# Cosine attention and a GELU layer on one core: the order of the squares in the first batch, and row sums with one chunk halved by queries

## The chip, the core and the metric

The kernel runs on one core of one Trainium2 chip. The time is that of the device in microseconds, the median of several executions. A profile is one execution taken by the hardware profiler.

## What is computed

There are 8 batches of 12 heads, 448 positions and 64 numbers per head. The queries q and keys k are divided by their norms, scores are divided by tau = 0.1, a softmax is taken over the keys, and the values v are averaged with it. The heads side by side (768 numbers for each of 8 x 448 = 3584 tokens) then go through two matrix products with a GELU between them:

```python
q_n = q / (np.linalg.norm(q, axis=-1, keepdims=True) + 1e-06)
k_n = k / (np.linalg.norm(k, axis=-1, keepdims=True) + 1e-06)
attn = np.exp(np.matmul(q_n, k_n.transpose(0, 1, 3, 2)) / tau)   # the reference takes the row maximum off first
out = np.matmul(attn / np.sum(attn, axis=-1, keepdims=True), v)
x = out.transpose(0, 2, 1, 3).reshape(3584, 768)
h = x @ w_in                                  # 768 x 2048
result = (0.5 * h * (1 + erf(h / sqrt(2)))) @ w_out   # 2048 x 768
```

## The kernel before

**Tiles.** Four heads make a "quad" (`g`, three to a batch, 24 in all). A quad's q and k lie in one tile of 128 partitions: two heads (`h`) on the partition halves, two pairs of them (`s`) on the free axis, and the 448 positions as 7 chunks of 64 (`c`). A "unit" is what is normalised at once: units 0 and 1 are the two halves of quad 0, unit `u` from 2 on is quad `u - 1`.

**From q and k to scores.** For each unit: `square` (L147) squares q and k, `reduce` (L158, VectorE) adds the squares up, `logs` and `roots` (L169, L174, ScalarE) take the root as exp(0.5 ln x), `inverses` (L183) adds 1e-6 (on VectorE in the first batch, on GpSimd later) and takes the reciprocal on VectorE, `scale` (L200) multiplies q and k with it on GpSimd or VectorE into bf16, and the result is transposed, in the first batch by TensorE with a copy by VectorE (`transposes` L214, `copies` L227), later by a DMA that SyncE issues (L220). `scores` (L236) are 64x64 matmuls, four of which run side by side in the array; `exps` (L250, ScalarE) take the exponential of two banks at a time (128 x 896).

**From exponentials to x.** `sums` (L259) multiplies each chunk of exponentials with a matrix of ones. In later batches that matrix has 32 columns, so that four such matmuls stand side by side in the array, in column strips `r` = 0, 32, 64 and 96: for `s` = 0 and 1, even chunks go into one strip and odd chunks into the other, and the two are added afterwards (`inverted` L296). `turned` (L291) transposes the sums, `inverted` takes reciprocals, `spread` (L312) spreads them out again, and `normalise` (L317) multiplies them into the output of `values` (L274, 64x64 matmuls), all on VectorE. `both` (L321) issues the whole of this for one quad.

**Order.** Nothing is scheduled by a planner: each engine runs its instructions in the order in which the program issues them. `attention_first` (L401) is the first batch, written out by hand. `attention` (L581) is a later batch: its scores are cut into eight `group`s (L575) of two or three passes over three pairs of PSUM banks (`group_pairs`, L573), and between them `run` (L586) issues matmuls of the second layer of the batch before (`second_pieces`, L339; 16 of them make one half row block, which VectorE then copies out, L352). `plan` (L583) gives the numbers of these filling matmuls: six runs, 96 in all in batches 1, 3, 5 and 7, and 128 in batches 2, 4 and 6. In `attention`, `both` of the batch's first quad follows group 2, that of the second follows group 5, and that of the third follows the last run. Three pairs of banks serve scores and, in turn, the values: pair 0 for the first quad, pair 1 for the others. `first` (L621) is the first layer of a batch with its GELUs; it begins with `scale` and `transposes` for the next batch.

`upto(f, n)` (L390) calls `f` for all numbers below `n` that have not been done. In `attention`, `upto(root, 2 * b + 5)` (L617) computes the norms of the next batch's first two quads: logs, roots and inverses, ahead of the last run.

Of the kernel before, what the change touches and what calls it, by code (L numbers as in the profile page):

```python
# [16 lines left out]
def kernel(  # L17
# [17 lines left out]
    nc = tc.nc  # L35
    B, H, S, D = q.shape
    C = S // D
# [35 lines left out]
    ones = consts.tile([128, 32], BF16)  # L73
# [25 lines left out]
    def mm_tile(name, shape=(128, 512), dtype=F32, aside=None):  # L99
        t = ps_mm.tile(list(shape), dtype, tag=f"mm{turn[0] if aside is None else turn[0] ^ aside}", name=name)  # L100
        if aside is None:
            turn[0] ^= 1
        return t
# [10 lines left out]
    groups = [[n] for n in range(NQ + 2)] + [[NQ + 2, NQ + 3]]  # L114
# [4 lines left out]
    qk_t, v_t, sq_t, nq_t, rn_t, qkb_t, qkT_t, pt_t = {}, {}, {}, {}, {}, {}, {}, {}  # L119
# [27 lines left out]
    def square(u, parts=None):  # L147
        g, s0, s1 = units[u]
        if g not in sq_t:
            sq_t[g] = sqp.tile([128, 2, 2, C, D], F32, tag="sq", name=f"sq{g}")  # L150
        sq, t = sq_t[g][:, :, s0:s1], qk_t[g][:, :, s0:s1]
        for eng, part in parts or ((nc.gpsimd, slice(0, 2)),):
            if eng is nc.scalar:
                eng.activation(sq[:, part], t[:, part], AF.Square)
            else:
                eng.tensor_tensor(sq[:, part], t[:, part], t[:, part], ALU.mult)  # L156

    def reduce(u, part=slice(0, 2)):  # L158
        g, s0, s1 = units[u]
        sq = sq_t[g][:, :, s0:s1]  # L160
        n, j = place[u]
        if n not in nq_t:
            nq_t[n] = nrm.tile([128, len(groups[n]), 2, s1 - s0, C], F32, tag="nq", name=f"nq{n}")
        nq = nq_t[n][:, j]
        nc.vector.tensor_reduce(nq[:, part], sq[:, part], mybir.AxisListType.X, ALU.add)  # L165
# [3 lines left out]
    def logs(n):  # L169
        nq = nq_t.pop(n)  # L170
        ln_t[n] = nrm.tile(list(nq.shape), F32, tag="lq", name=f"lq{n}")
        nc.scalar.activation(ln_t[n], nq, AF.Ln, bias=tiny)

    def roots(n):  # L174
        ln = ln_t.pop(n)
        if n <= NQ:
            sr_t[n] = root2[n % len(root2)][:, :math.prod(shapes[n])]
            nc.scalar.activation(sr_t[n][:, :, 0], ln.rearrange("p j i s c -> p (j i s c)"), AF.Exp, scale=0.5)
        else:
            sr_t[n] = nrm.tile(list(ln.shape), F32, tag="sr", name=f"sr{n}")  # L180
            nc.scalar.activation(sr_t[n], ln, AF.Exp, scale=0.5)  # L181

    def inverses(n):  # L183
        sr = sr_t.pop(n)
        shape = [128] + shapes[n]
        se = nrm.tile(shape, F32, tag="se", name=f"se{n}")
        if n <= NQ:
            nc.vector.tensor_reduce(se.rearrange("p j i s c -> p (j i s c)"), sr, mybir.AxisListType.X, ALU.add)
        else:
            nc.gpsimd.tensor_scalar(se, sr, 1e-6, None, ALU.add)  # L190
        rn = nrm.tile(shape, F32, tag="rn", name=f"rn{n}")
        nc.vector.reciprocal(rn, se)  # L192
        rn_t[n] = rn
# [20 lines left out]
    def transposes(u, i=None):  # L214
        g, s0, s1 = units[u]
        qkb = qkb_t[g]
        if g not in qkT_t:
            qkT_t[g] = qkTp.tile([128, 2, C, 128], BF16, tag="qkT", name=f"qkT{g}")
        if i is None:
            nc.sync.dma_start_transpose(out=qkT_t[g].rearrange("p i c s -> p (i c) s"),  # L220
                                        in_=qkb.rearrange("p i c s d -> p (i c s d)"))
            return
        tp = tp_t[u, i] = mm_tile(f"tp{u}_{i}", (128, C, 128), BF16)
        for c in range(C):
            nc.tensor.transpose(tp[64 * s0:64 * s1, c, :], qkb[:, i, c, s0:s1].rearrange("p s d -> p (s d)"), ident)  # L225
# [31 lines left out]
    bank_t = {}  # L257

    def sums(g, chunks=range(C)):  # L259
        for c in chunks:  # L260
            if c == 0:
                bank_t[g, "sm"] = ps_acc.tile([128, 512], F32, tag="sm", name=f"sm{g}") if g < NQ else \
                    mm_tile(f"sm{g}", aside=0)
            for s in range(2):
                if g < NQ:
                    nc.tensor.matmul(bank_t[g, "sm"][64 * s:64 * (s + 1), :S],  # L266
                                     lhsT=ones2.rearrange("p a h r -> p (a h r)"), rhs=pt_t[g, s, c],
                                     start=(c == 0), stop=(c == C - 1), tile_position=(0, 64 * s))
                    continue
                r = 32 * (2 * s + c % 2)  # L270
                nc.tensor.matmul(bank_t[g, "sm"][r:r + 32, :S], lhsT=ones, rhs=pt_t[g, s, c],  # L271
                                 start=(c < 2), stop=(c >= C - 2), tile_position=(0, r))

    def values(g, chunks=range(C), p=None):  # L274
        for c in chunks:
# [15 lines left out]
    def turned(g):  # L291
        tr = rcp.tile([128, NB, 32], F32, tag="tr", name=f"tr{g}")
        nc.vector.transpose(tr.rearrange("p b r -> p (b r)"), bank_t.pop((g, "sm"))[:, :S])  # L293
        bank_t[g, "tr"] = tr.rearrange("p b (k r) -> p k b r", k=2)

    def inverted(g):  # L296
        tr = bank_t.pop((g, "tr"))
        if g < NQ:
            su = tr[:, :, :, 0]
        else:  # L300


            for j in range(4):
                o = j ^ 1
                nc.vector.tensor_reduce(tr[32 * j:32 * (j + 1), :, :, 1], tr[32 * o:32 * (o + 1), :, :, 0:1],  # L305
                                        mybir.AxisListType.X, ALU.add)
            su = rcp.tile([128, 2, NB], F32, tag="su", name=f"su{g}")
            nc.vector.tensor_reduce(su, tr[:, :, :, 0:2], mybir.AxisListType.X, ALU.add)
        rc = bank_t[g, "rc"] = rcp.tile([128, 2, NB], F32, tag="rc", name=f"rc{g}")
        nc.vector.reciprocal(rc, su)  # L310
# [6 lines left out]
    def normalise(g, h):  # L317
        b, n = divmod(g, NQ)
        nc.vector.tensor_tensor(x_t[b][:, 2 * n + h, :], bank_t.pop((g, h))[:, :S], rs_t.pop((g, h)), ALU.mult)  # L319

    def both(g, p):  # L321
        sums(g)
        turned(g)
        inverted(g)
        spread(g, 0)
        spread(g, 1)
        values(g, p=p)
        normalise(g, 0)
        normalise(g, 1)
# [58 lines left out]
    done = {}  # L388

    def upto(f, n, last=None):  # L390
        last = {load_qk: NG, load_v: NV, root: len(groups), load_wi: 4, load_wo: 4}.get(f, NU)
        while done.get(f, 0) < min(n, last):
            done[f] = done.get(f, 0) + 1
            f(done[f] - 1)
# [6 lines left out]
    def attention_first():  # L401
        x_t[0] = xp.tile([128, KD, S], BF16, tag="x", name="x0")
        DV, AC, GP = nc.vector, nc.scalar, nc.gpsimd
        Q, K = slice(0, 1), slice(1, 2)
# [8 lines left out]
        roots(0)  # L413
        square(1, ((GP, K),))
        inverses(0)
        square(2, ((AC, Q),))
        scale(0, ((GP, 0),))
        reduce(1, K)
        reduce(2, Q)
        logs(1)  # L420
        scale(0, ((GP, 1),))
        spin(1)
        transposes(0, 0)
        roots(1)
        square(2, ((AC, K),))
        upto(load_v, 2)
        inverses(1)
# [2 lines left out]
        copies(0, 0)  # L430
        square(3, ((AC, Q),))
        copies(0, 1)
        square(3, ((AC, K),))
        spin(2)
        scores(0, ((0, 0), (0, 1)))
        reduce(2, K)
# [8 lines left out]
        exps(0, ((0, 2), (0, 3)))  # L445
        scores(0, ((0, 4), (0, 5)))
        upto(load_wi, 1)
        transposes(1, 0)
        copies(1, 1)
        logs(2)  # L450
# [129 lines left out]

    def attention(b, fill):  # L581
        fill = list(fill)
        plan = {96: (20, 12, 14, 12, 16, 22), 128: (24, 18, 20, 18, 22, 26)}[len(fill)]  # L583
        parts = iter(plan)

        def run():  # L586
            for _ in range(next(parts)):
                fill.pop(0)()

        x_t[b] = xp.tile([128, KD, S], BF16, tag="x", name=f"x{b}")  # L590
        g0, nu = b * NQ, (b + 1) * NQ + 1
        run()
        for n in (nu - 1, nu):
            upto(scale, n)
            upto(transposes, n)
        group(b, 1)
        upto(square, nu + 1)
        run()
        group(b, 2)
        both(g0, 0)  # L600
        upto(load_v, b + 3)
        if b == 1:
            upto(load_qk, g0 + NQ + 2)
        group(b, 3)
        upto(square, nu + 2)
        run()
        group(b, 4)
        upto(reduce, nu + 1)
        upto(load_qk, g0 + NQ + 3)
        run()  # L610
        group(b, 5)
        both(g0 + 1, 1)
        group(b, 6)
        run()
        group(b, 7)
        upto(reduce, nu + 2)
        upto(root, 2 * b + 5)  # L617
        run()
        both(g0 + 2, 1)

    def first(b):  # L621
        sb, hf = divmod(b, 2)
# [68 lines left out]
    fill = []  # L691
    for b in range(B):
# [12 lines left out]
        fill = [f for t, ni in todo if t not in tail for f in second_pieces(sb, t, ni)]  # L705
# [38 lines left out]
```

## Time and profile before

| what | value |
|---|---|
| median of 5 runs | 420.47 us (420.31 to 420.82) |
| the profiled execution's own time | 420.82 us |
| its span, first to last instruction | 419.1 us |
| what lies around the span | 1.7 us |
| TensorE busy | 410.8 us, 98% |
| ScalarE busy | 245.3 us, 59% |
| VectorE busy | 191.6 us, 46% |
| GpSimd busy | 166.4 us, 40% |
| row sums of later batches (L271) | 294 matmuls in 21 quads, 20.2 us |
| exponentials (L253) | 168 of 916 ns |

A line of the page's list of groups names the source line, engine, operation, tiles (written <- read), the shape and the count, then the busy time and the mean ns of one, then the time for which the engine had been idle before it and what ended that. A line of the timeline gives the start, the duration, the same names, and in square brackets the idle time before it and its releaser. The recorded duration of a matmul contains a modelled end; how densely TensorE works is read from the starts.

### The profile page before, as it was taken

The page shows a single profiled execution, that of the slowest core. Times are in us where ns is not written, and L with a number is a line of the kernel's source. Part 1 is how long each engine was busy: PE and PEld are TensorE (multiplying, and loading weights), DVE is VectorE, ACT ScalarE, POOL GpSimd, SP SyncE. Part 2 cuts the span into 40 slices and gives each one's busy share as a digit, 9 for nine tenths or more (in the row PEclk, how much of TensorE's full clock was granted, in tenths as well). Part 3 has the DMA queues.
Part 4 walks back from the last instruction along what each step waited for, and adds up shares of the span by engine and source line. Part 5 has one row for each costly group of instructions (what it writes and reads, how often), then busy time and mean ns, then how long its engine had stood idle before and what let it go on. Part 6 is the DMA issues. An engine that isn't in the chain of part 4 may idle for free.

```text
span 419.1 us, 8166 instructions
## 1 busy us (share of the span) xinstructions
PE 410.8 (98%) x3462; PEld 212.7 (51%) x3462; DVE 191.6 (46%) x381; ACT 245.3 (59%) x356; POOL 166.4 (40%) x113
## 2 busy tenths in 40 slices
PE   7899999999999999999999999999999999999996
PEld 3344545555555555554555555555555555555564
DVE  5897318820577107750277504861166511561021
ACT  5895697347663578734865359635866348844300
POOL 4898815440906309180542706372180802000000
PEclk9999999999999999999999999999999999999999
DMA  8999998490475806674191922957076510430033
GB/s 283 270 252 206 205 240 226 116 255 10 86 187 107 232 2 110 168 150 152 19 238 56 205 96 39 198 122 219 2 142 168 105 25 0 83 76 1 2 77 76
DMA packets 66516, 54.53 MB, mean 130 GB/s; under 512 B 38576, under 2 KB 61488, under 8 KB 66480
## 3 DMA queue, kind: packets, MB, share of 16 engines
q1 hardware_dynamic: 53984, 41.79, 39.0%
q0 software_dynamic: 12112, 11.80, 17.5%
q8 instruction: 27, 0.44, 0.4%
q10 hardware_dynamic: 384, 0.43, 0.3%
q14 instruction: 9, 0.07, 0.1%
HBM read 45.61 MB, written 11.01 MB: 135 GB/s over the span
## 4 chain that ended last, share of the span: by engine, by line
PE 44%; issue 31%; POOL 21%; DVE 2%; POOLq 0%; ACT 0%
PE hp L633 17%; PE op L348 15%; POOL sq L156 10%; POOL qkb L208 9%; PE st L246 4%; PE o L285 4%; PE sm L271 2%; PE op L363 1%; POOL v L141 1%; POOL wi L377 1%; DVE nq L165 1%; PE sm L266 1%; POOL se L190 1%; PE tp L225 0%; DVE x L319 0%
## 5 line engine op out<-in xcount | busy, mean ns | idle before, releaser
L253 ACT ACTIVATE pt<-st 128x896 bf16<-128x896 f32 x168 | 142.5, 916 | 41.0 <-PE st L246 40.5
L348 PE MATMUL op<-wo,g 128*128 128x384 bf16 x864 | 147.9, 327 | 0.0
L633 PE MATMUL hp<-x,wi 128*128 128x448 bf16 x768 | 146.8, 353 | 0.0
L669 ACT ACTIVATE g<-hp 128x448 bf16<-128x448 f32 x128 | 66.6, 546 | 100.1 <-PE hp L633 99.7
L348 PEld LDWEIGHTS <-g 128*128 128x128 bf16 x864 | 81.1, 98 | 63.7 <-issue 13.2
L633 PEld LDWEIGHTS <-wi 128*128 128x128 bf16 x768 | 74.5, 98 | 71.4 <-issue 2.9
L208 POOL TENSOR_TENSOR qkb<-qk,rn 128x896 bf16<-128x896 f32 (+1 forms) x48 | 77.9, 1650 | 10.1 <-DVE rn L192 10.0
L156 POOL TENSOR_TENSOR sq<-qk 128x1792 f32<-128x1792 f32 (+2 forms) x23 | 67.8, 2950 | 10.8 <-DMA qk<-in_k_dram 10.6
L190 POOL TENSOR_SCALAR se<-sr 128x28 f32<-128x28 f32 (+1 forms) x14 | 4.4, 312 | 164.5 <-ACT sr L181 164.5
L165 DVE TENSOR_REDUCE nq<-sq 128x28 f32<-128x1792 f32 (+2 forms) x30 | 48.7, 1636 | 26.1 <-POOL sq L156 26.1
L352 DVE COPY ot<-op 128x384 f32<-128x384 f32 x54 | 28.9, 540 | 58.5 <-PE op L348 58.5
L192 DVE RECIPROCAL rn<-se 128x28 f32<-128x28 f32 (+2 forms) x18 | 6.9, 384 | 98.9 <-POOL se L190 98.7
L246 PE MATMUL st<-qkT 64*64 64x448 bf16 x672 | 48.0, 358 | 0.9 <-DVE qkT L230 0.6
L285 PE MATMUL o<-pt,v 64*64 64x448 bf16 x672 | 36.9, 352 | 0.0
L246 PEld LDWEIGHTS <-qkT 64*64 64x64 bf16 x672 | 18.4, 105 | 25.7 <-issue 17.9
L314 DVE STREAM_TRANSPOSE rs<-rc 128x448 f32<-128x448 f32 x48 | 28.2, 625 | 0.8
L293 DVE STREAM_TRANSPOSE tr<-sm 128x448 f32<-128x448 f32 x24 | 15.6, 650 | 27.4 <-PE sm L271 26.8
L319 DVE TENSOR_TENSOR x<-o,rs 128x448 bf16<-128x448 f32 x48 | 27.0, 599 | 0.6 <-DVE rn L192 0.3
L285 PEld LDWEIGHTS <-v 64*64 64x64 bf16 x672 | 17.6, 106 | 16.0 <-issue 7.5
L271 PE MATMUL sm<-pt,ones 128*32 128x448 bf16 x294 | 20.2, 355 | 0.6 <-DVE ot L352 0.6
L305 DVE TENSOR_REDUCE tr<-tr 32x28 f32<-32x28 f32 x84 | 16.5, 197 | 1.6
L271 PEld LDWEIGHTS <-ones 128*32 128x32 bf16 x294 | 7.8, 95 | 11.5 <-issue 7.9
(44 smaller groups left out, 121.5 us busy)
## 6 DMA issues: line engine op xcount, KB each, us to landing
out_dram<-ot SPq DMA_DIRECT2D x54, 192.0 KB, 2.8
qk<-in_q_dram SPq DMA_DIRECT2D x23, 448.0 KB, 5.8
qk<-in_k_dram SPq DMA_DIRECT2D x23, 448.0 KB, 6.4
v<-in_v_dram POOLq DMA_DIRECT2D x7, 672.0 KB, 11.2
wi<-in_moe_w_in_dram POOLq DMA_DIRECT2D x8, 384.0 KB, 10.3
wo<-in_moe_w_out_dram POOLq DMA_DIRECT2D x4, 768.0 KB, 12.7
qk<-in_q_dram SPq DMA_DIRECT2D x2, 224.0 KB, 3.5
v<-in_v_dram POOLq DMA_DIRECT2D x1, 448.0 KB, 7.8
```

Of the source, the lines that this page charges most:

```text
L156: eng.tensor_tensor(sq[:, part], t[:, part], t[:, part], ALU.mult)
L165: nc.vector.tensor_reduce(nq[:, part], sq[:, part], mybir.AxisListType.X, ALU.add)
L208: eng.tensor_tensor(qkb[:, i, :, s0:s1].rearrange("p c s d -> p s c d"), t[:, i, s0:s1], rn[:, i].to_broadcast([128, s1 - s0, C, D]), ALU. ...
L246: nc.tensor.matmul(st[cols, n, :S], lhsT=qkT[rows, 1, c, cols], rhs=qkT[rows, 0, :, cols], start=True, stop=True, tile_position=(64 * s, 6 ...
L253: nc.scalar.activation(pt[:, :m], st[:, :m, :S], AF.Exp, scale=inv_tau)
L271: nc.tensor.matmul(bank_t[g, "sm"][r:r + 32, :S], lhsT=ones, rhs=pt_t[g, s, c], start=(c < 2), stop=(c >= C - 2), tile_position=(0, r))
L285: nc.tensor.matmul(bank_t[g, h][cols, :S], lhsT=v_t[g][rows, s, c, :], rhs=pt_t[g, s, c][rows], start=(c == 0), stop=(c == C - 1), tile_po ...
L314: nc.vector.transpose(rs, bank_t[g, "rc"][:, h].to_broadcast([128, NB, 32]))
L348: nc.tensor.matmul(ps[:, :NH], lhsT=g_t[sb][:, kf, t * 128:(t + 1) * 128], rhs=wo[:, kf, ni * NH:(ni + 1) * NH], start=(kf == 0), stop=(kf ...
L352: nc.vector.tensor_copy(ot[:, ni * NH:(ni + 1) * NH], ps[:, :NH])
L633: nc.tensor.matmul(hps[m], lhsT=wi[:, kd, m * 128:(m + 1) * 128], rhs=x_t[b][:, kd, :], start=(kd == 0), stop=(kd == KD - 1))
L669: nc.scalar.activation(g_t[sb][:, m, hf * S:(hf + 1) * S], hps.pop(m), AF.Gelu)
```

## The change

Three things are edited.

In `sums`, the chunk 2 of later batches is halved by queries: columns 0 to 223 go into one strip and columns 224 to 447 into the other, so that 16 matmuls replace 14 and each strip takes in three and a half chunks; chunks 3 to 6 alternate again.

In `attention_first`, the squares of q of unit 2 (quad 1) are issued on ScalarE after `roots(1)` and no longer ahead of it, their sum `reduce(2, Q)` moves from ahead of `inverses(1)` to behind the two copies of unit 0, and the squares of k of unit 3 (quad 2) move from ScalarE to GpSimd, behind the first load of `w_in`.

In `attention`, the plan with 96 pieces has 13 and 13 pieces in its second and third run instead of 12 and 14; and the norms of the next batch are split: logs and roots stay ahead of the last run, inverses follow `both` of the third quad.

```diff
@@ sums
-                r = 32 * (2 * s + c % 2)
-                nc.tensor.matmul(bank_t[g, "sm"][r:r + 32, :S], lhsT=ones, rhs=pt_t[g, s, c],
-                                 start=(c < 2), stop=(c >= C - 2), tile_position=(0, r))
+
+                half = 2
+                for i in range(2) if c == half else ((c - (c > half)) % 2,):
+                    r = 32 * (2 * s + i)
+                    cols = slice(i * S // 2, (i + 1) * S // 2) if c == half else slice(0, S)
+                    nc.tensor.matmul(bank_t[g, "sm"][r:r + 32, cols], lhsT=ones, rhs=pt_t[g, s, c][:, cols],
+                                     start=(c < 2), stop=(c >= C - 2), tile_position=(0, r))
@@ attention_first
         roots(0)
         square(1, ((GP, K),))
         inverses(0)
-        square(2, ((AC, Q),))
         scale(0, ((GP, 0),))
         reduce(1, K)
-        reduce(2, Q)
         logs(1)
         scale(0, ((GP, 1),))
         spin(1)
         transposes(0, 0)
         roots(1)
+        square(2, ((AC, Q),))
         square(2, ((AC, K),))
...
         square(3, ((AC, Q),))
         copies(0, 1)
-        square(3, ((AC, K),))
+        reduce(2, Q)
         spin(2)
...
         upto(load_wi, 1)
+        square(3, ((GP, K),))
         transposes(1, 0)
         copies(1, 1)
@@ attention
-        plan = {96: (20, 12, 14, 12, 16, 22), 128: (24, 18, 20, 18, 22, 26)}[len(fill)]
+        plan = {96: (20, 13, 13, 12, 16, 22), 128: (24, 18, 20, 18, 22, 26)}[len(fill)]
...
         upto(reduce, nu + 2)
-        upto(root, 2 * b + 5)
+        n = 2 * b + 4
+        if n < len(groups):
+            logs(n)
+            roots(n)
         run()
         both(g0 + 2, 1)
+        if n < len(groups):
+            inverses(n)
+            done[root] = n + 1
```

## The prediction

> **What bounds the kernel now.** I read the page first, then the waits, then the timeline engine by engine at the four places that the diff touches. From the page:
>
> ```profile
> span 419.1 us, 8166 instructions
> PE 410.8 (98%) x3462; PEld 212.7 (51%) x3462; DVE 191.6 (46%) x381; ACT 245.3 (59%) x356; POOL 166.4 (40%) x113
> PE   7899999999999999999999999999999999999996
> ```
>
> TensorE (PE) is full but for the first slices, so a later batch gets shorter only where TensorE has fewer columns to stream or waits less. The first batch is different: up to about 25 us TensorE waits for the chain of squares, norms, scaling and transposes. VectorE's timeline there:
>
> ```profile
> 9.54 0.17 DVE L188 TENSOR_REDUCE se<-root 128x14 f32<-128x28 f32 x1
> 9.75 0.24 DVE L192 RECIPROCAL rn<-se 128x14 f32<-128x14 f32 x1
> 9.90 1.13 DVE L230 COPY qkT<-tp 64x896 bf16<-64x896 bf16 x2
> 10.96 2.06 DVE L165 TENSOR_REDUCE nq<-sq 128x14 f32<-128x896 f32 x2
> 13.05 0.63 DVE L230 COPY qkT<-tp 64x896 bf16<-64x896 bf16 x1
> 14.29 0.63 DVE L230 COPY qkT<-tp 64x896 bf16<-64x896 bf16 x1 [0.61 <-PE tp L225]
> ```
>
> and all engines a little later:
>
> ```profile
> 14.97 0.94 PE L246 MATMUL st<-qkT 64*64 64x448 bf16 x8 [0.23 <-DVE qkT L230]
> 15.58 3.35 ACT L253 ACTIVATE pt<-st 128x896 bf16<-128x896 f32 x4 [0.38 <-PE st L246]
> 15.61 2.58 POOL L208 TENSOR_TENSOR qkb<-qk,rn 128x896 bf16<-128x896 f32 x1 [2.01 <-DVE rn L192]
> 19.53 0.38 PE L246 MATMUL st<-qkT 64*64 64x448 bf16 x4 [0.34 <-DVE qkT L230]
> ```
>
> The copy at 14.29 releases the scores of unit 1, these the exponentials; behind the copy VectorE makes the norms of unit 2 (rn at 15.19), GpSimd scales with them until 18.19, and the scores at 19.53 wait for what follows. VectorE's only slack ahead of that copy is the 0.61. TensorE and VectorE in batch 3, around the first quad's sums, and VectorE and TensorE before the third quad's sums of batch 1:
>
> ```profile
> 158.28 0.95 PE L246 MATMUL st<-qkT 64*64 64x448 bf16 x12
> 159.16 0.93 PE L271 MATMUL sm<-pt,ones 128*32 128x448 bf16 x14
> 160.03 1.52 PE L285 MATMUL o<-pt,v 64*64 64x448 bf16 x28
> 164.23 0.76 PE L246 MATMUL st<-qkT 64*64 64x448 bf16 x12
> ```
>
> ```profile
> 75.19 2.00 DVE L165 TENSOR_REDUCE nq<-sq 128x28 f32<-128x1792 f32 x1
> 78.31 0.50 DVE L192 RECIPROCAL rn<-se 128x56 f32<-128x56 f32 x1 [1.12 <-POOL se L190]
> 78.73 0.98 DVE L352 COPY ot<-op 128x384 f32<-128x384 f32 x2
> ```
>
> ```profile
> 79.28 0.93 PE L271 MATMUL sm<-pt,ones 128*32 128x448 bf16 x14 [0.16 <-DVE ot L352]
> ```
>
> A copy whose bank had been full since about 76.4 stands behind the reciprocal, which waits 1.12 us for GpSimd; TensorE's sums wait for that copy.
>
> **What the Trainium skill says.** "TensorE: Matmul & The Clock Gate" (Back-to-back issue gap) gives N/2.4 + 2.5 ns between starts; the trace's starts agree: 189 ns for 448 columns, 163 for 384, 56 for 128. For 224 columns, which the trace lacks, that is an estimated 96 ns. The same section warns of more when weights are loaded for each matmul (81 ns at 128); the trace, with a load for each, does not show that. "TensorEngine Tiling (Array Packing)" (Key Properties) says that a change of tiling mode drains the array; here the start after such a change comes 281 to 292 ns on, so about 95 ns more. "SBUF — State Buffer" (Who interferes with whom) says that a VectorE operation with two SBUF inputs and a GpSimd operation that reads SBUF lock each other out, and that a reduction never contends. The trace agrees: the scaling at 15.61 took 2.58 instead of 1.69 us beside VectorE's scaling of 1.09, and GpSimd's scalings of 0.95 beside reductions kept their length.
>
> **Halved chunk.** A quad's sums are rounds of four matmuls side by side: starts 0, 189, 378, 567 ns, the last round half empty, then the values at 864. With chunk 2 halved they are 448, 224, 448, 448 columns: 189 - 96 = 0.093 us less for each of 21 quads, 1.96 in all, if nothing else is late. Two more matmuls and weight loads lie inside rounds whose members start 2 to 4 ns apart, so I cost them at nothing; should the short round wait for its weight loads (97 ns each), 0.093 shrinks toward 0, the other bound.
> What is late next: the *first* quad's last chunk is the first pass of group 2. In batch 1 its scores start at 60.12, its exponential at 60.56, and the sum of it only at 61.52, 1.40 after the scores and 0.13 after TensorE was ready. Batches 2, 4 and 6 show the same 313 ns gap. There a shorter sum only waits longer: 0. For the *second* quad the values may start 0.05 earlier than the first exponential of group 5 needs, fine, but group 6 then meets the last exponential of group 5: of 0.093 some 0.02 is lost (exponential ends 71.75, scores at 71.87). For the *third* quad nothing is in the way. So 7 x 0.073 + 7 x 0.093 = **-1.16 us** (the first quads of batches 3, 5, 7 are under the plan).
>
> **Plan 13, 13.** In batches 3, 5 and 7 the third pass of group 2 waits 0.17 for an exponential (start gap 357 instead of 189). One more filling matmul (0.163) ahead of group 2 covers that. But the one taken out stood between the sums and group 4, whose third pass needs pair 0, that is the end of `normalise` of the first quad. From the scores of the last chunk this takes 1.40 to its sum, 0.40 to VectorE's transpose, 4.38 on VectorE (61.93 to 66.31) and 0.05 back: 6.24. TensorE's own way was 6.31 in batch 1 (60.12 to 66.43), 6.36 in batches 3, 5 and 7; with one filling matmul less it is at most 6.20, so it now waits. Group 2 starts 0.163 later and the stretch shrinks only by 0.07 and 0.12: **+0.10 and 3 x 0.04, about +0.21 us**, and nothing is left of the halving there. Bounds: -0.5 if VectorE's chain isn't in the way, +0.65 if all four pieces are lost.
>
> **Inverses behind `both`.** Ahead of the third quad's sums the start gap is 485, 557 and 554 ns in batches 1, 3 and 5, against 256 in batches 2 and 4 where the copy comes in time. Without the reciprocal in its way the copy starts after the reduction (77.19) and is done by 77.8, over 1 us before the sums: 0.229 + 0.301 + 0.298 = **-0.83 us**. The price: rn comes after `normalise` (84.61) instead of 78.82, and what depends on it moves by some 6.3 us in six batches: four scalings (6.63 us), the square behind them, two DMA transposes and four loads on SyncE's queue. No store stands behind them there. Scores of the next batch need the first transpose at 99.86; I get 84.61 + 0.65 (rn and wait) + 3.34 (two scalings) + 4.1 (median to landing) = 92.7, 7.1 us of cover, so 0. Nor is anything late that uses the square (needed by ScalarE at some 105, done by 97) or the loads (landing about 102, used at 109).
>
> **First batch.** ScalarE loses two squares (0.95 each) ahead of the first exponential: it can start at 11.85, not 12.23, as its scores are ready. VectorE skips `reduce(2, Q)` (8.54 to 9.62), but then waits for the roots at 9.21 and for TensorE's second transposition (copy at 10.42 as before), so the time is lost. From 10.96 it now has three reductions at 0.99 instead of two: to 14.01. The copies of unit 1 follow at 14.05 and 14.63, done at 15.25 instead of 14.92. The 0.61 of slack is used up, 0.34 is not covered. Scores of unit 1, ScalarE's exponentials, rn of unit 2 (15.87) and all behind it move by **+0.34 us**. GpSimd squares k of unit 3 from 13.60 to 15.29 (1.69, as its square at 19.46), in a gap of 2.01, beside reductions and copies from PSUM only; it is done before rn at 15.87 and before VectorE's scaling. From 22.8 on TensorE is packed until the first layer at 34.16, so nothing gives the 0.34 back. Bounds: -0.38 if the earlier exponential is what counts; +1.3 if the copies hold up GpSimd's square (1.69 plus 1.25 of copies), so that the scalings of unit 2 wait and collide.
>
> **Sum.** -1.16 + 0.21 - 0.83 + 0.34 = -1.44 us. The profiled execution took 420.82 (span 419.05, 1.77 around it): 419.4. The median shown is 420.47, 0.35 lower: **419.0 us**. A change under 0.2% (0.84 us) is about what a measurement can't tell from none, so "faster" ends at 419.63.
>
> **Rivals.**
> A, more is gained (17%): the first batch gains the 0.38 of the earlier exponentials: 420.47 - 1.16 + 0.21 - 0.83 - 0.38 = 418.3, and 417.6 with the plan at -0.5 too. For it: ScalarE waited for data at 11.37. Against: VectorE's copies, not ScalarE, release the scores at 14.97.
> B, less is gained (15%): GpSimd's square is held up (+1.3 for +0.34): 420.0; or the short round takes as long as a full one (+1.16, the change not doing what it says): 420.2. Against the first: copies beside scalings at 45.3 didn't lengthen them. Against the second: 56 ns for 128 columns.
> C, slower (8%): the later scalings push the transposes into other traffic. The cover of 7.1 us is gone when a transpose takes more than 11.2 to land; median 4.1, but the longest in this trace is 10.1. At 11.6 each of six batches loses 0.4: 419.0 + 2.4 = 421.4. It is slower than before from 11.45 on. Against: SyncE's loads follow the transposes, so the DMA queues are nearly idle then.
> The forecast has 60%, from 418.5 to 419.6. The range 418.0 to 420.4 leaves out C and the far end of A. Faster takes the forecast and A: 0.77; same takes B: 0.15; slower 0.08.
>
> **What would show it.** Right: 16 sums per quad with the values 0.77 instead of 0.864 after their start in second and third quads; no wait of the sums for L352; the reciprocal of the norms after `normalise`; group 4 of batches 1, 3, 5, 7 waiting about 0.1 for x; the copy of unit 1 ending at 15.25 and the first layer starting at 34.5. Wrong: a first layer at or before 34.16 or after 34.8; short rounds near 189 ns; TensorE waiting for transposed qkT at the start of a later batch.

## The result, and the profile after

The changed kernel takes 419.29 us (median of 43 runs, 418.97 to 419.96) against 420.55 for the kernel before (80 runs): 1.26 us or 0.3% faster, ratio 0.9967 with a 95% interval from 0.9959 to 0.9976. The prediction said 419.0, with a range from 418.0 to 420.4. Medians in this document are over all executions of a kernel, while a ratio leaves out only those more than 1.5% above the fastest of the kernel, so that long executions below that still count in it.

The page of the changed kernel:

```profile
span 417.3 us, 8250 instructions
PE 409.3 (98%) x3504; PEld 211.7 (51%) x3504; DVE 191.8 (46%) x381; ACT 244.5 (59%) x355; POOL 168.1 (40%) x114
PE   7899999999999999999999999999999999999996
```

Line numbers are those of each kernel's own file; from `sums` on they are 4 to 10 higher in the changed one. TensorE is as full as before; it has 1.5 us less to do and to wait for. Where the time went is read from the starts of the first layer (the first `hp` matmul of each batch) in the two traces:

| stretch | before | changed | difference |
|---|---|---|---|
| start of the span to the first layer of batch 0 | 34.16 | 33.85 | -0.30 |
| to the first layer of batch 1 | 47.44 | 47.18 | -0.26 |
| batches 2, 4, 6, each | 51.50 | 51.37 | -0.135 |
| batches 3 and 5, each | 46.78 | 46.40 | -0.38 and -0.37 |
| batch 7 | 46.47 | 46.40 | -0.08 |
| from there to the last 16 matmuls | 38.12 | 38.12 | 0.00 |

The last 16 matmuls (128 columns each) are the end point here; the start of the very last one is 0.84 us behind it in both kernels. From the first layer of batch 0 on, 380.09 us became 378.59: -1.49. The first stretch is another matter: the loads of q and k landed earlier in this execution (k of unit 1 at 5.28 us and not at 5.87, q of unit 2 at 6.53 and not at 7.53). GpSimd's first multiplication (squares of k of unit 1), ahead of which the two kernels differ in nothing, ended at 7.96 us before and at 7.37 here, 0.59 earlier. From that end to the first layer it is 26.20 us before and 26.48 now: +0.28. VectorE's timeline of the first batch, after:

```profile
8.65 0.18 DVE L188 TENSOR_REDUCE se<-root 128x14 f32<-128x28 f32 x1 [0.62 <-ACT root L178]
8.86 0.24 DVE L192 RECIPROCAL rn<-se 128x14 f32<-128x14 f32 x1
9.02 0.55 DVE L230 COPY qkT<-tp 64x896 bf16<-64x896 bf16 x1
9.83 0.62 DVE L230 COPY qkT<-tp 64x896 bf16<-64x896 bf16 x1 [0.26 <-PE tp L225]
10.37 3.05 DVE L165 TENSOR_REDUCE nq<-sq 128x14 f32<-128x896 f32 x3
13.46 1.17 DVE L230 COPY qkT<-tp 64x896 bf16<-64x896 bf16 x2
```

Three reductions now stand in one piece ahead of the copies of unit 1, and there is no idle time between these copies any more. All engines behind them:

```profile
14.68 0.94 PE L246 MATMUL st<-qkT 64*64 64x448 bf16 x8
15.29 3.35 ACT L253 ACTIVATE pt<-st 128x896 bf16<-128x896 f32 x4 [1.19 <-PE st L246]
15.31 2.59 POOL L208 TENSOR_TENSOR qkb<-qk,rn 128x896 bf16<-128x896 f32 x1 [0.58 <-DVE rn L192]
19.24 0.38 PE L246 MATMUL st<-qkT 64*64 64x448 bf16 x4 [0.34 <-DVE qkT L230]
```

ScalarE, which started its exponentials early, waits 1.19 us here where it had waited 0.38. TensorE in batch 3 around the first quad:

```profile
157.75 0.79 PE L246 MATMUL st<-qkT 64*64 64x448 bf16 x12
158.47 1.05 PE L275 MATMUL sm<-pt,ones 128*32 128x448 bf16 x16
159.45 1.52 PE L289 MATMUL o<-pt,v 64*64 64x448 bf16 x28
163.49 0.86 PE L246 MATMUL st<-qkT 64*64 64x448 bf16 x12
```

The scores ahead of the sums are short now (0.79 for 0.95), but the sums take until the values start 0.98 instead of 0.87, and the scores at 163.49 have a wait inside them (0.86 for 0.76). VectorE, then TensorE, at the third quad of batch 1:

```profile
74.92 2.00 DVE L165 TENSOR_REDUCE nq<-sq 128x28 f32<-128x1792 f32 x1
76.84 0.54 DVE L356 COPY ot<-op 128x384 f32<-128x384 f32 x1
78.91 0.56 DVE L356 COPY ot<-op 128x384 f32<-128x384 f32 x1 [1.53 <-PE op L352]
...
83.99 0.48 DVE L192 RECIPROCAL rn<-se 128x56 f32<-128x56 f32 x1
```

```profile
78.81 0.85 PE L275 MATMUL sm<-pt,ones 128*32 128x448 bf16 x16
79.58 1.52 PE L289 MATMUL o<-pt,v 64*64 64x448 bf16 x28
```

The copy runs at once after the reduction, the sums wait for nothing, and the values follow 0.777 us after their start (0.864 before). What was put off is put off without harm: GpSimd's scalings and SyncE's first transpose of that batch,

```profile
84.62 6.62 POOL L208 TENSOR_TENSOR qkb<-qk,rn 128x896 bf16<-128x896 f32 x4 [6.61 <-DVE rn L192]
```

```profile
87.98 4.80 SPq L220 DMA_TRANSPOSE qkT<-qkb  x2
```

start 5.7 us later than before; with a median of 4.0 us to landing the first is there at 92.0, and the scores that read it start at 99.30 without a wait.

### The profile page after: what moved, and what is told of

It is laid out like the page before. It is cut to its first block, busy times and chain, and to the rows that moved or that the text cites. A ratio compares the mean times of both kernels' runs of the same rounds, so it can differ in the third digit from the quotient of the medians.

```text
span 417.3 us, 8250 instructions
## 1 busy us (share of the span) xinstructions
PE 409.3 (98%) x3504; PEld 211.7 (51%) x3504; DVE 191.8 (46%) x381; ACT 244.5 (59%) x355; POOL 168.1 (40%) x114
## 4 chain that ended last, share of the span: by engine, by line
PE 93%; POOL 4%; issue 2%; DVE 0%; POOLq 0%
PE hp L643 35%; PE op L352 35%; PE st L246 9%; PE o L289 8%; PE sm L275 4%; POOL qkb L208 1%; PE op L367 1%; POOL sq L156 1%; POOL wi L381 1%; PE sm L266 1%; POOL v L141 0%; PE tp L225 0%; DVE last L370 0%; POOL ident masks.py:199 0%; POOL ident masks.py:197 0%
## 5 line engine op out<-in xcount | busy, mean ns | idle before, releaser
L156 POOL TENSOR_TENSOR sq<-qk 128x1792 f32<-128x1792 f32 (+2 forms) x24 | 69.5, 2897 | 10.2 <-DMA qk<-in_k_dram 10.0
L275 PE MATMUL sm<-pt,ones 128*32 128x448 bf16 (+1 forms) x336 | 19.3, 332 | 0.0
```

The lines of the kernel that those rows point to most:

```text
L275: nc.tensor.matmul(bank_t[g, "sm"][r:r + 32, cols], lhsT=ones, rhs=pt_t[g, s, c][:, cols], start=(c < 2), stop=(c >= C - 2), tile_position ...
```

## The experiments

In the table, "q landed" is when the load of q of unit 2 was complete, "from the multiplication" is the time from the end of GpSimd's first multiplication to the first layer of batch 0, and "late" that from there to the start of the last 16 matmuls (the recorded expectations call this "to the last matmul"), all from the trace of the one execution that was profiled. e1 to e4, e5 to e8 and e9 to e12 were measured on three chips; the kernel before had medians of 420.65, 420.59 and 420.57 us there.

| kernel | first batch | plan | other | q landed | from the multiplication | late | median us | ratio to before, interval |
|---|---|---|---|---|---|---|---|---|
| before | old | 12, 14 | | 7.53 | 26.20 | 380.09 | 420.55 | |
| e12 (before again) | old | 12, 14 | | 7.13 | 26.03 | 380.09 | 420.25, one run | |
| changed | new | 13, 13 | | 6.53 | 26.48 | 378.59 | 419.29 | 0.9967, 0.9959 to 0.9976 |
| e1 | old | 13, 13 | | 9.13 | 32.28 | 378.57 | 419.22 | 0.9947, 0.9921 to 0.9973 |
| e2 | new | 12, 14 | | 7.81 | 26.55 | 378.17 | 419.15 | 0.9946, 0.9922 to 0.9969 |
| e3 | new | 13, 13 | inverses early | 7.95 | 26.48 | 379.32 | 420.11 | 0.9988, 0.9971 to 1.0005 |
| e4 | new | 13, 13 | whole chunks | 6.92 | 26.48 | 379.52 | 420.33 | 0.9995, 0.9972 to 1.0019 |
| e5 | k of unit 3 alone | 13, 13 | | 6.87 | 25.97 | 378.59 | 419.18 | 0.9976, 0.9946 to 1.0007 |
| e6 | new | 13, 13 | first quads whole | 9.07 | 26.81 | 378.71 | 419.28 | 0.9958, 0.9938 to 0.9977 |
| e7 | old | 12, 14 | | 6.71 | 25.92 | 378.17 | 418.72 | 0.9960, 0.9941 to 0.9978 |
| e8 | k of unit 3 alone | 12, 14 | | 6.94 | 25.88 | 378.17 | 418.48 | 0.9949, 0.9921 to 0.9977 |
| e9 | old, q of quad 1 late | 12, 14 | | 8.71 | 31.85 | 378.17 | 423.46 | 1.0002, 0.9956 to 1.0047 |
| e10 | new, q of quad 1 late | 12, 14 | | 8.18 | 26.48 | 378.17 | 419.08 | 0.9976, 0.9955 to 0.9997 |
| e11 | new, a sum later | 12, 14 | | 8.63 | 26.54 | 378.16 | 418.67 | 0.9941, 0.9919 to 0.9963 |

The late column repeats to 0.03 us between kernels that share their late batches (378.57 to 378.59 three times; 378.16 or 378.17 six times; 380.09 twice), so a tenth is read there with ease. The intervals of the ratios in the experiments are 0.3 to 0.9% wide, that is 1.4 us and more; they decide nothing that is argued below.

**e1: the first batch undone.**

```diff
@@ attention_first: as in the kernel before
+        square(2, ((AC, Q),))        # ahead of scale(0), logs(1)
+        reduce(2, Q)                 # ahead of logs(1)
-        square(2, ((AC, Q),))        # behind roots(1)
+        square(3, ((AC, K),))
-        reduce(2, Q)                 # behind the copies of unit 0
-        square(3, ((GP, K),))
```

> The changed kernel with the first batch in its old order. My theory: the new order costs 0.3 us, because three reductions instead of two stand ahead of the copies of unit 1 on VectorE; the earlier first layer in the profile of the changed kernel (33.85 for 34.16) came from loads that landed 0.58 earlier there, in code that both kernels share. So this one is 0.3 us faster than the changed kernel: 419.0 us, 1.5 under the kernel before; from the end of GpSimd's first multiplication (squares of k of unit 1) to the start of the first layer I expect 26.20 us as before, against 26.48 in the changed kernel. Rival: the new order is a gain of 0.3 us, as the two starts of the first layer say by themselves: then 419.6 us, and 26.8 for that stretch or a first multiplication that is itself later because of the order.

The median is 419.22, 0.07 below the changed kernel. That decides nothing, and the stretch of 26.20 was not seen: in the execution that was profiled, q of unit 2 landed only at 9.13 us, the logarithms of unit 1 stood behind it on ScalarE, and the granted clock fell in the second and third slice,

```profile
PEclk9579999999999999999999999999999999999999
```

so that the first layer began at 39.85. This wasn't in either theory, and it led to e9 and e10.

**e2: the plan undone.**

```diff
-        plan = {96: (20, 13, 13, 12, 16, 22), 128: (24, 18, 20, 18, 22, 26)}[len(fill)]
+        plan = {96: (20, 12, 14, 12, 16, 22), 128: (24, 18, 20, 18, 22, 26)}[len(fill)]
```

> The changed kernel with 12 and 14 filling matmuls in the second and third run. My theory: 13 and 13 makes group 4 of batches 1, 3, 5 and 7 wait for x of the first quad, 0.11 us in batch 1 and some 0.06 in the others; undone, the kernel is 0.3 us faster: 419.0 us, third pass of group 4 without a wait (189 ns after the second one, not 276), third pass of group 2 in batches 3, 5, 7 waiting 0.17 again. Rival: the plan gained the 0.5 us of the third pass of group 2: then 419.8 us.

The late batches are 0.43 shorter than in the changed kernel: 0.11 in each of batches 1, 3, 5 and 7. The third pass of group 4 follows the second by 189 ns again. The theory holds, with a larger figure: in batches 3, 5 and 7 some 0.04 of the 0.11 is the halving of the first quad's sums (values 0.82 after the sums' start, before 0.86), which does pay when group 2 isn't pushed back.

**e3: the inverses ahead of the last run again.**

```diff
-        n = 2 * b + 4
-        if n < len(groups):
-            logs(n)
-            roots(n)
+        upto(root, 2 * b + 5)
         run()
         both(g0 + 2, 1)
-        if n < len(groups):
-            inverses(n)
-            done[root] = n + 1
```

> The changed kernel with the inverses ahead of the last run again. My theory: sums of the third quad wait again for the copy behind the reciprocal, 0.23 us in batch 1 and 0.30 in 3 and 5, none in 2, 4, 6 and 7: 0.83 us slower, 420.1 us. Rival 1: the later scalings and transposes cost something that the saving hides, then less than 0.8, down to 0. Rival 2: the copy waits for the reduction of the squares and not for the reciprocal, then 0.

0.73 us in the late batches, 0.82 in the median. VectorE at the third quad of batch 1:

```profile
75.06 2.00 DVE L165 TENSOR_REDUCE nq<-sq 128x28 f32<-128x1792 f32 x1
78.19 0.50 DVE L192 RECIPROCAL rn<-se 128x56 f32<-128x56 f32 x1 [1.12 <-POOL se L190]
78.61 1.00 DVE L356 COPY ot<-op 128x384 f32<-128x384 f32 x2
```

The copy stands behind the reciprocal again, and the sums start 469 ns after the last filling matmul in batch 1 and 532 in batch 3, instead of 256 and 255. Both rivals fall; batches 2, 4 and 6 are unchanged (51.37 each).

**e4: whole chunks in all sums.**

```diff
-                half = 2
-                for i in range(2) if c == half else ((c - (c > half)) % 2,):
-                    r = 32 * (2 * s + i)
-                    cols = slice(i * S // 2, (i + 1) * S // 2) if c == half else slice(0, S)
-                    nc.tensor.matmul(bank_t[g, "sm"][r:r + 32, cols], lhsT=ones, rhs=pt_t[g, s, c][:, cols],
+                r = 32 * (2 * s + c % 2)
+                nc.tensor.matmul(bank_t[g, "sm"][r:r + 32, :S], lhsT=ones, rhs=pt_t[g, s, c],
```

> The changed kernel with sums of whole chunks. My theory: 0.087 us for each second and third quad, 14 in all, less 0.04 for each second quad whose group 6 meets the last exponential of group 5; nothing for first quads, where the last chunk's exponential ends the sums: 14 x 0.087 - 7 x 0.04 = 0.95 us slower, 420.2 us. Rival 1: all 21 quads gain, 1.8 us: 421.1. Rival 2: the gain is lost at the next wait, 0: 419.3.

0.92 us in the late batches (0.12 to 0.14 in each), 1.04 in the median. In batch 2, whose second quad shows it best, the sums and values of e4 start at 119.22 and 120.08, those of the changed kernel at 119.02 and 119.79, so that the values start 0.087 sooner after the sums. Of this the group that follows, group 6, gives back 0.039: in the changed kernel its second pass waits 15 ns for the last exponential of group 5, and the filling matmul behind it comes 316 ns after that pass where it comes 292 after it in e4.

**e6: halved sums in second and third quads only.**

```diff
-                half = 2
+                half = 2 if g % NQ else C
```

> The changed kernel with whole chunks in the first quad of each batch, halved ones in the second and third. My theory: the first quad's sums end with the exponential of its last chunk, so halving is worth nothing there: each batch takes the same time within 0.01 us as in the changed kernel, 419.3 us. Rival: the halving helps there as elsewhere, 7 x 0.09 = 0.6 us slower, 419.9.

419.28 us against 419.29, and batches 2 to 7 within 0.014 us of the changed kernel. Under the plan with 13 and 13 the halving of first quads is worth nothing: their last chunk's sum waits for its exponential. (In batch 1 this profile is 0.11 longer; its second pass of group 2 waited 0.23 for the transposed q and k of quad 4, a DMA's landing.)

**e7: the two gains alone.** The kernel before with the halved chunk and the late inverses:

```diff
@@ against the changed kernel: attention_first as before, and
-        plan = {96: (20, 13, 13, 12, 16, 22), ...
+        plan = {96: (20, 12, 14, 12, 16, 22), ...
```

> The kernel before with the halved chunk and the inverses behind the third quad, and nothing else. My theory: it keeps the two gains and drops the two losses: 0.28 us of the first batch and 0.43 us of the plan under the changed kernel, so 418.6 us; 26.20 us from the end of GpSimd's first multiplication to the first layer. Rival: the new order of the first batch is a gain: 419.2 us and a longer stretch than 26.48.

418.72 us, as the theory said, 0.43 below e2, from which it differs only in the first batch. TensorE in batch 3:

```profile
156.99 0.95 PE L246 MATMUL st<-qkT 64*64 64x448 bf16 x12
157.87 0.89 PE L275 MATMUL sm<-pt,ones 128*32 128x448 bf16 x16
158.69 1.52 PE L289 MATMUL o<-pt,v 64*64 64x448 bf16 x28
162.90 0.76 PE L246 MATMUL st<-qkT 64*64 64x448 bf16 x12
```

The wait is back in the scores ahead of the sums (0.95), and gone from the sums and from group 4: from the first scores to group 4 it is 5.91 us with 14 filling matmuls, 5.74 in the changed kernel with 13. The moved matmul took 0.16 out of the wait in the scores of group 2. All of that came back in the sums, whose values start 0.98 after them and not 0.82 as here, and group 4 waits some 0.10 on top.

**e5 and e8: of the first batch only k of unit 3.** In both, q of unit 2 and its sum are where they were before:

```diff
@@ attention_first, against the kernel before
-        square(3, ((AC, K),))
...
         upto(load_wi, 1)
+        square(3, ((GP, K),))
```

> The changed kernel with one part of its first batch undone: squares of q of unit 2 and their sum stand ahead of the inverses of unit 1 again; only the squares of k of unit 3 stay on GpSimd. My theory: the loss of the first batch is the third reduction ahead of the copies of unit 1, so it goes, and the earlier exponential now shows: the copies of unit 1 end 0.65 earlier than in the kernel before, but GpSimd's square (until 15.29 on that kernel's clock) holds up the scaling of unit 2, so that 0.2 are left. From the end of GpSimd's first multiplication to the first layer: 26.0 us (26.20 before, 26.48 changed), 0.5 under the changed kernel: 418.8 us. Rival: the loss comes from GpSimd's square itself, by collision; then it stays, 26.5 us.

> The halved chunk, the inverses behind the third quad, the old plan, and of the first batch only the squares of k of unit 3 on GpSimd. If the two losses add up with that gain: 0.43 + 0.5 under the changed kernel, 418.4 us. Rival: GpSimd's square collides with the scalings of unit 2 and the first batch is as in the changed kernel, 418.9 us.

25.97 and 25.88 from the multiplication: the loss of the first batch is gone though GpSimd's square is still there, so the square isn't its cause. What was undone is the place of the square of q of unit 2 and of its sum `reduce(2, Q)`: two reductions stand ahead of the copies of unit 1 again (2.06 us in e5) where the changed kernel has three (3.05). The second of these copies ends 6.74 us after the multiplication in e5 and 7.25 in the changed kernel, and these 0.51 us reach the first layer in full. In all profiles at full clock but e11's, whichever order they have, the first layer starts 19.22 to 19.24 us after the end of that copy. The order acts through this one point. But it is no gain over the old order where the loads come early (25.92 in e7), as ScalarE then doesn't wait for k of unit 3. The medians, 419.18 and 418.48, are too noisy to say more.

**e12: the kernel before, profiled again.**

> The kernel before, unchanged, for a second profile of it. Theory: its late batches repeat to 0.01 us (380.09 from the first layer to the last matmul), while the first batch differs with the landing of its loads by some tenths, 25.9 to 26.2 after GpSimd's first multiplication. Rival: the first batch is the same too, 26.20 from that point and 34.16 from the start, and then the difference to the changed kernel is one of the order.

26.03 and a first layer at 33.54 instead of 34.16. The late batches repeat, the first batch doesn't: it moves by 0.6 us with the landing of its loads, for the same program. So the -0.30 in the table of the result can't be put down to the change.

**e9 and e10: q of quad 1 loaded behind k.** The same swap in both, with the old first batch in e9 and the new one in e10:

```diff
@@ load_qk
-            for i, src in enumerate((q, k)):
+            for i, src in ((1, k), (0, q)) if g == 1 else ((0, q), (1, k)):
```

> Halved chunk, inverses behind the third quad, old plan, old first batch, and the two loads of quad 1 in the other order, k ahead of q, so that q of unit 2 lands later. Theory from the profiles so far: in the old order the squares of q of unit 2 stand on ScalarE ahead of the logarithms of unit 1, so a late q holds up unit 1 and with it all transposes; I expect q about 1 us later and the first layer 0.7 us later than with the old load order (25.92 after GpSimd's first multiplication there), so about 26.6 and 419.4 us. Rival: the order on ScalarE doesn't matter, since the logarithms wait for the squares of k by GpSimd anyway: 25.9 and 418.7 us.

> The same loads, k of quad 1 ahead of q, with the new first batch (and the old plan). Theory: the logarithms of unit 1 no longer stand behind q of unit 2, so the late load costs at most 0.1 us: 26.5 to 26.6 after GpSimd's first multiplication, 419.1 to 419.2 us. The two kernels with the late load are then alike in time, where the old order was 0.4 to 0.5 faster with the early load. Rival: it loses as much as the old order, 27.2 and 419.8 us.

423.46 us against 419.08. ScalarE's timeline of e9, then of e10:

```profile
8.73 0.95 ACT L154 ACTIVATE sq<-qk 128x896 f32<-128x896 f32 x1 [2.08 <-DMA qk<-in_q_dram]
9.59 0.29 ACT L172 ACTIVATE lq<-nq,tiny 128x14 f32<-128x14 f32 x1
9.91 0.22 ACT L178 ACTIVATE root<-lq 128x14 f32<-128x14 f32 x1
10.03 2.62 ACT L154 ACTIVATE sq<-qk 128x896 f32<-128x896 f32 x3
```

```profile
8.12 0.31 ACT L172 ACTIVATE lq<-nq,tiny 128x14 f32<-128x14 f32 x1 [1.59 <-DVE nq L165]
8.46 0.21 ACT L178 ACTIVATE root<-lq 128x14 f32<-128x14 f32 x1
8.59 2.61 ACT L154 ACTIVATE sq<-qk 128x896 f32<-128x896 f32 x3
11.17 1.73 ACT L253 ACTIVATE pt<-st 128x896 bf16<-128x896 f32 x2
```

In e9 ScalarE stands 2.08 us before the square that waits for q, and the logarithms of unit 1, whose data were there, come at 9.59; in e10 they come at 8.12 and nothing waits for the load, which landed 0.53 earlier there. The prediction for e10 held. For e9 I had expected 0.7 us and got that only in part: 5 of its 14 executions lie between 418.9 and 419.5, where 0.7 over e7 is, and 9 between 422.2 and 426.3. The profiled one is of the second kind, and there TensorE's clock fell to half. The same two stretches of e9 and e10 (start and end, length, then busy time and instructions of each engine, then the clock):

```profile
14.00:20.00 6.00, 6.00 (x31) 2.25 (x28) 4.03 (x7) 3.62 (x6) 2.55 (x2) 0.50 1.14 266
20.00:26.00 6.00, 6.00 (x39) 2.40 (x40) 2.82 (x5) 3.18 (x5) 5.91 (x7) 0.50 1.02 219
```

```profile
14.00:20.00 6.00, 5.13 (x45) 2.09 (x44) 5.25 (x11) 4.20 (x8) 5.40 (x5) 1.00 1.14 262
20.00:26.00 6.00, 5.62 (x82) 2.65 (x81) 5.87 (x8) 5.67 (x7) 5.96 (x7) 1.00 1.10 271
```

At a clock of 0.50 TensorE did 39 matmuls in 20 to 26 us and not 82.

e1 and e6 show the same with the loads as they were. Up to the first layer they differ in the order alone, and in the executions that were profiled their loads landed almost alike: q of unit 2 at 9.13 in e1 and 9.07 in e6, the next three at 10.34, 11.57 and 13.80 and at 10.23, 11.48 and 13.80. ScalarE in e1 (old order), then in e6 (new order):

```profile
9.16 0.95 ACT L154 ACTIVATE sq<-qk 128x896 f32<-128x896 f32 x1 [2.45 <-DMA qk<-in_q_dram]
10.01 0.29 ACT L172 ACTIVATE lq<-nq,tiny 128x14 f32<-128x14 f32 x1
```

```profile
8.22 0.31 ACT L172 ACTIVATE lq<-nq,tiny 128x14 f32<-128x14 f32 x1 [1.65 <-DVE nq L165]
8.56 0.21 ACT L178 ACTIVATE root<-lq 128x14 f32<-128x14 f32 x1
9.09 0.95 ACT L154 ACTIVATE sq<-qk 128x896 f32<-128x896 f32 x1 [0.32 <-DMA qk<-in_q_dram]
```

In e6 the logarithms come 1.79 us sooner, TensorE never waits longer than 0.74 us from then to 20 us and keeps its full clock, and the first layer starts 26.81 us after the multiplication; in e1 TensorE waits 2.12 us (up to 12.11) and the first layer starts after 32.28.

That a late load delays unit 1 in the old order and hardly in the new one is shown; that the idle time which it leaves on TensorE (1.72 us at its longest in e9, up to 11.69) brings the lower clock is what the four traces suggest, and no run here varied that alone.

The medians hide what this is worth. Without e9 and e10, 9 of 67 executions of the experiments with the old first batch or its old place of q (e1, e5, e7, e8) took more than 422 us, as did 34 of 157 of the kernel before that ran beside the experiments; with the new first batch (e2, e3, e4, e6, e11) it was 3 of 87. In the result it was 4 of 80 before and none of 43. By the mean of all executions the change is worth 1.45 us (420.83 to 419.38), not 1.26. That late loads made these executions long is likely but not shown; of them only one of e1's was profiled.

**e11: the sum of q of unit 3 behind the scaling.**

```diff
@@ attention_first, against e2
-        reduce(3, Q)                 # ahead of the copies of unit 1
...
+        reduce(3, Q)                 # behind scale(2, ((DV, 1),))
         reduce(3, K)
```

> New first batch, old plan, and one more move: the sum of the squares of q of unit 3 goes from ahead of the copies of unit 1 to behind VectorE's scaling of unit 2. Theory: the three reductions ahead of the copies are the cost of the new order; with two, the copies of unit 1 end 0.6 earlier, and later copies give half of it back, as VectorE has one reduction more ahead of the copies of unit 2: 26.2 to 26.3 instead of 26.55 after GpSimd's first multiplication, 418.8 us where the kernel with 12 and 14 pieces had 419.15. Rival: nothing, since the copies of unit 2 are then late by as much: 26.5.

418.67 us (418.24 to 419.36 in 18 runs), 0.48 below e2 where 0.35 was expected. Its profiled execution doesn't show it: 26.54. ScalarE's second and third squares waited for loads there (0.18 and 0.31), so that the exponentials began at 11.94 and not at 11.1. VectorE:

```profile
10.57 2.06 DVE L165 TENSOR_REDUCE nq<-sq 128x14 f32<-128x896 f32 x2
12.66 0.63 DVE L230 COPY qkT<-tp 64x896 bf16<-64x896 bf16 x1
14.00 0.63 DVE L230 COPY qkT<-tp 64x896 bf16<-64x896 bf16 x1 [0.71 <-PE tp L225]
```

The first copy is 0.8 earlier than in the changed kernel, and the slack of the second is back; this time TensorE's transposes came late. From the end of the second copy to the first layer it is 19.48 us, 0.25 more than in the other profiles: this is what the theory said that the later copies give back. The profile shows the shorter reductions and the price, the median the gain that is left. e7, e8 and e11 beat both kernels by the median (418.5 to 418.7); the intervals of their ratios overlap each other and that of the changed kernel, so they aren't ranked. e11 has the new order, which a late q of unit 2 doesn't hold up.

## Why the prediction was right

**Halved chunk: right, a little too high.** The short round takes 95 to 96 ns, as estimated. But the change of tiling behind the last round comes 292 ns after a round of four and 286 after one of two, so a quad saves 0.087 and not 0.093; and where the last pass of a group of scores had to wait, the filling matmul behind it comes 24 ns later still (316 for 292; behind sums that had waited, the values come after 296), so that the second quad loses 0.039 and not 0.02. From e7: 7 x (2 x 0.087 - 0.039) = 0.945 us, where the prediction had 1.16; taking it out of the changed kernel cost 0.92 (e4). First quads of batches 1, 2, 4 and 6 gained nothing, as said: their sums take 1.008 us as before. Their rounds followed each other after 199, 189 and 323 ns before and after 200, 96, 189 and 227 ns now: what the short round gave is waited away at the last chunk.

**Inverses: right.** The gaps ahead of the third quad's sums went from 485, 557 and 554 to 256, 255 and 256 ns: 0.83 us. The cover of the transposes was 7.3 us, 7.1 by the prediction; rival C did not come, and the longest landing of a transpose in the changed kernel was 9.4.

**Plan: the sign and place right, the size somewhat low.** Group 4's third pass comes 276 ns after the second in batch 1 and 266 in batch 3 (189 before), and the stretch from the last chunk's scores to it is 6.23 us in batch 1 (59.98 to 66.21), 6.24 by the prediction. What was left out is again the 24 ns behind each wait. What remains of -1.49 for the plan, with -0.945 and -0.83 taken off, is +0.28, where the prediction had +0.21. Against a kernel that has the halving already the plan costs more, 0.43 (e2), as the first quads' sums of batches 3, 5 and 7 gain 0.04 each without it.

**First batch: right in mechanism.** The copies of unit 1 end at 14.63 here; with the 0.59 by which this execution was early that is 15.22, where the prediction had 15.25. The loss is 0.28 between the two profiles, 0.43 between the medians of e2 and e7, and 0.56 between the profiles of the changed kernel and e7, in both of which q of unit 2 came early (6.53 and 6.71); the prediction had 0.34, worked out on a profile in which q came at 7.53. A first layer at or before 34.16 was one of its signs of being wrong, and 33.85 was measured; that sign was tied to the landings of one profile, and counted from the multiplication the first layer is late as forecast. What its working missed is that the profile of before was one draw of the landings. It took ScalarE's waits for loads (1.04 for q of unit 2, 0.38 for k of unit 3) as fixed, and so saw in the new order only its price. The order decides what a late load holds up, and e1 beside e6 shows that this is worth more than the price, in the executions where q comes late: 5.5 us.

**The sum.** The medians moved by -1.26, where the prediction had -1.78 + 0.34 = -1.44. The late batches gained 0.29 less than forecast; what the medians leave for the first batch, +0.23, isn't a measurement of it but the remainder of -1.26 and -1.49. If it is taken as it stands, the first batch lost 0.11 less, and the two errors cancel in part: that the sum came within 0.18 is partly luck. Of the rivals, B's short round at full length is excluded by the 96 ns, its held-up square by e5, A's gain of the first batch by 26.48 for 26.20 and by e7, and C by the cover of 7.3 us.

**Price of the short round, and the lower clock.** The estimate of 96 ns for 224 columns from the Trainium skill ("TensorE: Matmul & The Clock Gate", Back-to-back issue gap) was measured. The same page (Part 1: The HAM clock gate, What's actually happening) puts the lower clock behind an idle window of some 3.4 us; in e9 the clock fell after waits of at most 1.72 us with matmuls between them. Here the measurement decides, and what the condition is stays open.

## What to carry to other kernels

When work is taken off a full engine, look up what ended last at that place and add the price of the next wait: of 21 shorter sums only 14 paid here, and a filling matmul moved away from one wait met another. In an in-order queue an instruction that waits for a load should not stand ahead of one whose data are there: a profile with an early load shows only what moving it costs, and a median hides the executions in which it pays. Before the first batch of two profiles is compared, line them up at the last point ahead of which the programs are the same.

## What the runs showed that I had not expected

One and the same program differed by 0.6 us in the start of the first layer (34.16 and 33.54), of which 0.46 stood at the end of the first multiplication already, behind the first loads, while the 380.09 us behind it repeated to 0.01. Where the last pass of a group of scores had waited, TensorE's next matmul of another tiling came 316 ns on, without a wait 292. And in the old order loads that landed 2.4 us later and more from q of unit 2 on (9.13 in e1 for 6.71 in e7) were followed by 13.7 us at half clock (12.14 to 25.80), so that the first layer came at 39.85 and not at 33.37.
